# Attention feeding a mixture of experts: turned rows in two buffers, gate columns inside the turning products, loads one by one

## The chip, the cores and the metric

The kernel runs on one core of a Trainium2 chip. The metric is the device time of one execution in microseconds, as the median of several runs. Engines: PE is the matrix engine (its weight loads are listed apart as PEld), DVE the vector engine, ACT the scalar engine, POOL the general engine, SP the engine that issues most DMA transfers. Each runs its own instructions in order, and engines wait for one another by semaphores. PE's array writes to PSUM banks, which DVE and ACT read.

## The reference

Attention over 8 batches, 12 heads, 448 positions and head size 64, with a mix over heads before the softmax and one after it, and then a layer of 8 experts in which each of the 3584 rows goes to the one expert with the largest logit:

```
scores = scale * q @ k.T                                # per batch and head
scores = einsum('bhij,hg->bgij', scores, w_pre)         # mix over heads
attn = softmax(scores)
attn = einsum('bhij,hg->bgij', attn, w_post)            # mix over heads
x = (attn @ v), heads side by side                      # 3584 x 768
logits = x @ w_gate                                     # 8 experts
e = argmax(logits); gate = softmax(logits)[e]
out = gate * (relu(x @ w1[e]) @ w2[e])
```

## The kernel before, in words

**Tiles, blocks and steps.** A batch's 448 queries are cut into four tiles of 120, 120, 120 and 88 queries, 32 tiles in all, and a tile into blocks of up to 20 queries: six blocks in a long tile, five in the short one, 184 in all. The attention stage runs one step per block, 23 steps per batch. What a step does is a list with a sort key for each entry; the list, and so the order on every engine, is written out by the function `at(u, key, what, ...)`, which puts a piece of work into step `u`. A step's pieces come from different tiles, since each tile's work is spread over some twenty steps.

**What one tile goes through.** `load_q` brings its queries (two DMAs of 64 partitions each) and `order_q` reorders them on POOL. `qk` computes the scores of one pair of heads (PE, bank `bs`), and ACT copies them to `si`. Six pairs are done in the six steps from eight steps before the tile's first block on. A short tile has five steps, so once per batch, seven times in all, two pairs fall into one step; the second has the sort key 7, at the step's end. `relayout` (two DMAs on SP, `sb<-si`) puts a block's scores of all heads side by side, three steps ahead of use. `mix` multiplies by the first head matrix (PE, banks `bm`), `top_of` takes the maximum (DVE) and `expo` the exponential (ACT). A step later `weigh` scales the second head matrix (POOL), and two steps later `post` multiplies (56 half records on PE, bank `bp`), and `spread` copies the result to `pt` (DVE). `av` multiplies by v (PE, bank `bx`) over the next tile's steps; `take_a` and `take_b` move its sums to `xt`.

**Turned rows.** `rows` turns `xt` by products with an identity, so that each token is a row, and multiplies it by the gate's columns, with two pairs of heads at a time. So a tile has three visits to `rows`; the first comes three steps after the tile's first `av`. A visit's turned rows stand in columns 360 and up of the two `bx` banks, whose columns below 360 `av` fills; the gate's sums of the three visits stand in the last 24 columns. `copy_x` (ACT, L393) copies turned rows to `xr`, of which there is one buffer, placed between the step's two exponentials. `logits` adds the gate's sums (DVE, L408), `choose` finds the expert, `count` and `dispatch` give each token its place, with a scatter from POOL (L471), and `store_x` writes `xr` to DRAM (`XD`, L399, on SP) in the step before the next tile's first visit.

**Loads.** k of the next batch (six DMAs) comes in steps 2 to 7 of a batch, v in steps 10, 12, 14 and 16, two DMAs each. All these, the q loads, the relayouts and the stores stand in one order on SP.

The expert stage behind it gathers rows by expert from `XD` and runs two layers.

Of the kernel before, what the change touches and what calls it, by code (L numbers as in the profile page):

```python
# [23 lines left out]
P = 128  # L24
# [16 lines left out]
def attn_moe_kernel(ctx, tc, qT, kT, v, w_pre, w_post, w_gate, w1, w2, out):  # L41
# [59 lines left out]
    def load_q(T):  # L101
        b, it, ni = geom[T][:3]
        qr = q_p.tile([P, NPAIR, IT], F32, name="qr", bufs=1)
# [3 lines left out]
        QR[T] = qr  # L107
# [23 lines left out]
    def load_v(b, cs=range(NJ)):  # L131
        for c in cs:
            for r in range(2):
                j0 = min(2 * c + r, NBLK - 1) * D
                nc.sync.dma_start(out=VT[b % 2][r * D:(r + 1) * D, c, :], in_=v[b, j0:j0 + D, :])
# [11 lines left out]
    load_q(0)  # L147
# [42 lines left out]
    wg = const.tile([P, NPAIR, NE], F32, name="wg")  # L190
    nc.scalar.dma_start(out=wg, in_=w_gate.rearrange("(c p) e -> p c e", p=P))
# [175 lines left out]
    LCOL = 512 - 3 * NE  # L367

    def rows(T, pairs, bank, col):
        if 0 in pairs:  # L370
            LG[T] = []
            XR[T] = x_p.tile([IT, NPAIR, 2, D], F32, name="xr")
        to = bank[:, :, col:col + len(pairs) * D].rearrange("p r (c x) -> p r c x", x=D)
        for k, h2 in enumerate(pairs):
            for cs in COLS:
                for r in range(2):
                    rs = slice(r * D, (r + 1) * D)
                    nc.tensor.matmul(out=to[cs, r, k, :], lhsT=xt[rs, h2, cs], rhs=ident[rs, rs],
                                     start=True, stop=True)
        lo = bank[:, :, LCOL + len(LG[T]) * NE:LCOL + (len(LG[T]) + 1) * NE]  # L380
        for k, h2 in enumerate(pairs):
            for cs in COLS:
                for r in range(2):
# [3 lines left out]
        LG[T].append(bank)  # L387


    def copy_x(T, pairs, bank, col):  # L390
        ni = geom[T][2]
        to = bank[:ni, :, col:col + len(pairs) * D].rearrange("p r (c x) -> p c r x", x=D)
        nc.scalar.copy(out=XR[T][:ni, pairs[0]:pairs[-1] + 1], in_=to)  # L393

# [10 lines left out]
    def logits(T):  # L405
        ni, bank, nv = geom[T][2], LG[T][0], len(LG[T])
        lg = LG[T] = sm_p.tile([IT, NE], F32, name="lgs")
        nc.vector.reduce_sum(out=lg[:ni], in_=bank[:ni, :, LCOL:LCOL + nv * NE]  # L408
                             .rearrange("p r (v e) -> p e r v", e=NE), axis=AX.XY)


    def choose(T):
        ni = geom[T][2]
        lg = LG.pop(T)
# [109 lines left out]
    for T in range(NTILE):  # L524
        b, it, ni = geom[T][:3]
        u0, n = ustart[T], len(geom[T][3])
        if T:
            at(max(u0 - QLEAD - 4, -1), 0, load_q, T)
            at(max(u0 - QLEAD - 2, -1), 0.1, order_q, T, 0)
            at(max(u0 - QLEAD - 1, -1), 0.1, order_q, T, 1)  # L530
# [19 lines left out]
        if T == NTILE - 1:  # L550
            O = T - 1

            def whole(T, g, banks):
                for h2 in range(3 * g, 3 * g + 3):
# [5 lines left out]
                    (take_b, T, 0, bank_m), (copy_x, O, (2, 3, 4, 5), bank_x, 0), (logits, O),  # L560
                    (choose, O), (weight, O), (store_x, O), (take_a, T, 1, banks_s),
                    (take_b, T, 1, banks_s), (count, O), (dispatch, O),
                    (rows, T, (0, 1, 2), bank_x, 0), (rows, T, (3, 4, 5), bank_x, 3 * D), (logits, T),
                    (choose, T), (weight, T), (copy_x, T, range(6), bank_x, 0), (store_x, T),
# [17 lines left out]
        for k, pairs in visits:  # L582
# [4 lines left out]
        at(ua + nn + 1, 2.2, logits, T)  # L587
# [4 lines left out]
        at(ua + nn + 2, 5.7, store_x, T)  # L592
# [4 lines left out]
    at(0, 0.5, load_v, 0)  # L597
# [275 lines left out]
```

## Time and profile before

| | us |
|---|---|
| median of 3 runs | 1406.04 |
| lowest and highest | 1405.06, 1407.02 |
| the profiled execution | 1402.59 |
| its span, first to last instruction | 1400.8 |
| PE busy (share of the span) | 1259.6 (90%) |
| DVE, ACT, POOL busy | 735.2 (52%), 657.1 (47%), 389.1 (28%) |

The profile is of one execution, and durations come from it. A busy PE is not a PE at its peak, since matmuls overlap. Idle time of an engine that is not the bottleneck costs nothing, and a share of the whole span averages over stages with different limits, so a stage is read by its own stretch of time. On this profile a step of the attention stage lasts about 3.4 to 10 us, as cut from one `spread` to the next.

### The profile page before, as it was taken

How to read it: one execution, taken by the hardware profiler on the slowest of the kernel's cores; microseconds unless marked ns; L12 is line 12 of the kernel's file. 1: busy time of each engine (PE TensorE's matmuls, PEld its weight loads, DVE VectorE, ACT ScalarE, POOL GpSimd, SP SyncE). 2: the span in 40 equal slices, each digit the busy share in tenths (PEclk: the TensorE clock that was granted, in tenths of full speed). 3: DMA queues.
4: the chain of work that ended last, by engine and by line, in shares of the span. 5: the costliest groups of instructions: out<-in, count | busy, mean ns of one | idle time of the engine just before them, and what ended most of it. 6: DMA issues, size and time to landing. Idle time of an engine off the chain costs nothing. (4 is left out here: it accounts for less than half of the span.)

```text
span 1400.8 us, 57280 instructions
## 1 busy us (share of the span) xinstructions
PE 1259.6 (90%) x25184; PEld 1082.5 (77%) x25184; DVE 735.2 (52%) x1492; ACT 657.1 (47%) x1421; POOL 389.1 (28%) x923
## 2 busy tenths in 40 slices
PE   5889989899888899899899867999999999999995
PEld 1577778777777777687688757989898989988985
DVE  1566757666656675576667655333333333342510
ACT  3556656565655565566566433333333333341510
POOL 3234334333423433343344222202020202020101
PEclk9999999999999999999999887999999999999998
DMA  4663554646536555454634427253433343452501
GB/s 137 185 198 115 172 174 147 182 141 171 170 129 170 153 166 155 135 183 138 184 129 163 144 62 241 77 180 138 132 131 139 125 147 125 140 188 72 165 1 42
DMA packets 116190, 201.21 MB, mean 144 GB/s; under 512 B 40658, under 2 KB 90018, under 8 KB 115924
## 3 DMA queue, kind: packets, MB, share of 16 engines
q1 hardware_dynamic: 108528, 172.38, 39.4%
q0 software_dynamic: 6064, 23.86, 4.6%
q8 instruction: 209, 3.42, 1.0%
q10 hardware_dynamic: 1332, 1.08, 0.3%
q14 instruction: 57, 0.47, 0.1%
HBM read 97.59 MB, written 23.06 MB: 86 GB/s over the span
## 5 line engine op out<-in xcount | busy, mean ns | idle before, releaser
L325 PEld LDWEIGHTS bx<-pt,vt 64*64 64x64 f32 x5952 | 294.4, 136 | 49.4 <-ACT xr L393 38.8
L252 PE MATMUL bm<-sb,Wpre 64*64 64x448 f32 x1440 | 325.8, 556 | 5.4 <-DMA sb<-si 4.6
L325 PE MATMUL bx<-pt,vt 64*64 64x120 f32 (+3 forms) x5952 | 302.2, 253 | 30.5 <-ACT xr L393 27.5
L258 DVE TENSOR_REDUCE st<-bm 128x1 f32<-128x448 f32 (+1 forms) x368 | 225.9, 623 | 162.8 <-PE bm L252 136.5
L264 ACT ACTIVATE et<-bm,st 128x448 f32<-128x448 f32 (+1 forms) x368 | 233.1, 636 | 93.8 <-DVE st L258 89.9
L295 PE MATMUL bp<-wp,et 60*64 60x60 f32 x10080 | 231.2, 225 | 30.4 <-issue 29.5
L306 DVE COPY pt<-bp 128x960 f32<-128x960 f32 (+1 forms) x184 | 216.3, 1175 | 73.9 <-PE bp L295 70.2
L295 PEld LDWEIGHTS bp<-wp,et 60*64 60x64 f32 x10080 | 207.1, 138 | 41.6 <-issue 38.6
L226 PE MATMUL bs<-kr,qq 64*64 64x448 f32 (+1 forms) x1536 | 207.1, 576 | 23.0 <-ACT si L228 13.2
L228 ACT COPY si<-bs 120x896 f32<-120x896 f32 (+1 forms) x192 | 173.6, 904 | 101.6 <-PE bs L226 99.5
L277 POOL TENSOR_SCALAR wp<-Wpost,st 128x60 f32<-128x60 f32 (+1 forms) x368 | 110.4, 312 | 301.3 <-DVE st L274 222.9
L729 POOL DMA_INDIRECT out<-y,ti x30 | 33.7, 1122 | 455.4 <-ACT xh L656 339.7
L252 PEld LDWEIGHTS bm<-sb,Wpre 64*64 64x64 f32 x1440 | 94.4, 138 | 84.0 <-issue 52.4
L701 PE MATMUL pm_h<-xh,ah 128*128 128x512 f32 (+1 forms) x384 | 146.0, 380 | 1.6 <-PEq L753 0.7
L701 PE MATMUL pm_h<-xl,ah 128*128 128x512 f32 (+1 forms) x384 | 145.1, 378 | 0.0
L701 PE MATMUL pm_h<-xh,al 128*128 128x512 f32 (+1 forms) x384 | 145.0, 378 | 0.0
L720 PE MATMUL pm_y<-bh,hh 128*128 128x384 f32 x480 | 127.8, 343 | 0.0
L720 PE MATMUL pm_y<-bl,hh 128*128 128x384 f32 x480 | 123.6, 336 | 0.0
L720 PE MATMUL pm_y<-bh,hl 128*128 128x384 f32 x480 | 121.1, 336 | 0.0
L705 DVE SCALAR_TENSOR_TENSOR hl<-pm_h,hh 128x512 fp32r<-128x512 f32 (+1 forms) x64 | 42.0, 657 | 134.5 <-ACT hh L704 134.4
L704 ACT ACTIVATE hh<-pm_h 128x512 fp32r<-128x512 f32 (+1 forms) x64 | 36.5, 571 | 147.9 <-PE pm_h L701 147.7
L725 DVE TENSOR_SCALAR y<-pm_y,tb 128x384 f32<-128x384 f32 x30 | 18.4, 614 | 155.4 <-PE pm_y L720 155.4
(106 smaller groups left out, 1626.8 us busy)
## 6 DMA issues: line engine op xcount, KB each, us to landing
sb<-si SPq DMA_DIRECT2D x360, 210.0 KB
wraw<-in_w SPq DMA_DIRECT2D x64, 384.0 KB
wraw<-in_w SPq DMA_DIRECT2D x46, 512.0 KB
vt<-in_v SPq DMA_DIRECT2D x64, 192.0 KB
kr<-in_kT SPq DMA_DIRECT2D x48, 224.0 KB
qr<-in_qT SPq DMA_DIRECT2D x48, 180.0 KB
XD<-xr SPq DMA_DIRECT2D x24, 360.0 KB
qr<-in_qT SPq DMA_DIRECT2D x16, 132.0 KB
```

The lines of the kernel that those rows point to most:

```text
L226: nc.tensor.matmul(out=bank_s[cs, r, :S], lhsT=QQ[T][hs, c, cs], rhs=KR[b, c][hs, :], start=True, stop=True)
L228: nc.scalar.copy(out=SI[T][:ni, 2 * c:2 * c + 2, :], in_=bank_s[:ni, :, :S])
L252: nc.tensor.matmul(out=bank_m[x][c * D:(c + 1) * D, :S], lhsT=Wpre[hs, :], rhs=SB[T, s][hs, c, :], start=True, stop=True)
L258: nc.vector.reduce_max(out=st[:top, 0, x:x + 1], in_=bank_m[x][:top, :S], axis=AX.X, negate=True)
L264: nc.scalar.activation(out=et[:top, x, :], in_=bank_m[x][:top, :S], func=AF.Exp, bias=st[:top, 0, x:x + 1], scale=1.0, accum_out=st[:top, ...
L277: nc.gpsimd.tensor_scalar(out=wp[:top, x, :], in0=Wpost[:top], scalar1=st[:top, 2, x:x + 1], scalar2=1.0, op0=ALU.mult, op1=ALU.mult)
L295: nc.tensor.matmul(out=bank_p[g * D:(g + 1) * D, n, o:o + nw], lhsT=et[hs, x, j * D:(j + 1) * D], rhs=wp[hs, x, :], start=True, stop=True)
L306: nc.vector.tensor_copy(out=to, in_=src[:, :2 * nh])
L325: nc.tensor.matmul(out=o, lhsT=VT[b % 2][rs, c, h * D:(h + 1) * D], rhs=i, start=(c == 0), stop=(c == NJ - 1))
L701: nc.tensor.matmul(out=ph[:, :n], lhsT=wx[:, fs], rhs=xx[:, kt, :n], start=(m == 0), stop=(m == 3 * NK1 - 1))
L705: nc.vector.scalar_tensor_tensor(out=hl[:, ft, :n], in0=ph[:, :n], scalar=0.0, in1=hh[:, ft, :n].bitcast(F32), op0=ALU.max, op1=ALU.subtract)
L720: nc.tensor.matmul(out=py[g][:, :384], lhsT=hx[:, kt, ts], rhs=wx[:, g * 384:(g + 1) * 384], start=(n == 0), stop=(n == 3 * NK2 - 1))
```

## The change

It has four parts. (1) `xr` gets two buffers, and `store_x` comes two steps later for all tiles but the last three. (2) `rows` multiplies by one operand `iw`, which holds 64 identity columns and 8 gate columns for each pair of heads, so a turning product has 72 columns and the gate's own products are gone. The gate's columns stand beside each pair's turned columns; `logits` adds them at each visit, and `choose` adds the three results. Two POOL copies fill `iw` at the start. (3) The loads of k, v and q are placed in single pieces: k in steps 1, 3, 4, 8, 9 and 12, v in steps 12, 13, 14, 15, 18, 20, 20 and 21, the halves of q in two steps, the first a step earlier than before. (4) The second score pair of a step gets the key 0.96 and so stands ahead of the step's mixes.

```diff
-    def load_q(T):
+    def load_q(T, half):
...
-        for half in range(2):
-            nc.sync.dma_start(out=qr[half * D:(half + 1) * D, :, :ni], in_=src[half])
+        nc.sync.dma_start(out=QR[T][half * D:(half + 1) * D, :, :ni], in_=src[half])
...
-    wg = const.tile([P, NPAIR, NE], F32, name="wg")
-    nc.scalar.dma_start(out=wg, in_=w_gate.rearrange("(c p) e -> p c e", p=P))
+    iw = const.tile([P, NPAIR, D + NE], F32, name="iw")
+    nc.scalar.dma_start(out=iw[:, :, D:], in_=w_gate.rearrange("(c p) e -> p c e", p=P))
+    for r in range(2):
+        rs = slice(r * D, (r + 1) * D)
+        nc.gpsimd.tensor_copy(out=iw[rs, :, :D],
+                              in_=ident[rs, rs].unsqueeze(1).to_broadcast([D, NPAIR, D]))
...
-            XR[T] = x_p.tile([IT, NPAIR, 2, D], F32, name="xr")
+            XR[T] = x_p.tile([IT, NPAIR, 2, D], F32, name="xr", bufs=2)
+            LG[T] = sm_p.tile([IT, NE, 3], F32, name="lg")
...
-                    nc.tensor.matmul(out=to[cs, r, k, :], lhsT=xt[rs, h2, cs], rhs=ident[rs, rs],
+                    nc.tensor.matmul(out=to[cs, r, k, :], lhsT=xt[rs, h2, cs], rhs=iw[rs, h2, :],
                                      start=True, stop=True)
-        lo = bank[:, :, LCOL + len(LG[T]) * NE:LCOL + (len(LG[T]) + 1) * NE]
-        for k, h2 in enumerate(pairs):
-            for cs in COLS:
-                for r in range(2):
-                    rs = slice(r * D, (r + 1) * D)
-                    nc.tensor.matmul(out=lo[cs, r, :], lhsT=xt[rs, h2, cs], rhs=wg[rs, h2, :],
-                                     start=(k == 0), stop=(k == len(pairs) - 1))
...
+    def logits(T, v, n, bank, col):
+        ni = geom[T][2]
+        nc.vector.reduce_sum(out=LG[T][:ni, :, v], in_=turned(bank, col, n)[:ni, :, :, D:]
+                             .rearrange("p r c e -> p e r c"), axis=AX.XY)
...
+        lg = sm_p.tile([IT, NE], F32, name="lgs")
+        nc.vector.reduce_sum(out=lg[:ni], in_=lg3[:ni, :, :nv], axis=AX.X)
...
-            at(max(u0 - QLEAD - 4, -1), 0, load_q, T)
...
+                at(max(u0 - QLEAD - 5 + half, -1), 0.01 * T, load_q, T, half)
...
-            for c in range(NPAIR):
-                at(u0 + 2 + c, 5.6, load_k, b + 1, c)
-            for c in range(NJ):
-                at(u0 + 10 + 2 * c, 5.6, load_v, b + 1, (c,))
+            for c, k in enumerate((1, 3, 4, 8, 9, 12)):
+                at(u0 + k, 5.6, load_k, b + 1, c)
+            for c, k in enumerate((12, 13, 14, 15, 18, 20, 20, 21)):
+                at(u0 + k, 5.6, load_v, b + 1, (c,))
...
-            at(u, 7 if u in scored and u >= 0 else 5, qk, T, c)
+            at(u, 0.96 if u in scored and u >= 0 else 5, qk, T, c)
...
+            at(ua + k, 2.2, logits, T, n3, 2, bank_x, 3 * IT)
...
-        at(ua + nn + 2, 5.7, store_x, T)
+        at(ua + nn + (4 if T < NTILE - 3 else 2), 5.7, store_x, T)
```

The order on SP, steps 10 to 15 of the third batch, before. `vt` are loads of v, `qr` of q, `sb` the relayouts and `XD` the store; x2 means two DMAs.

```order
L135 DMA vt_114<-in_v 64x768 x2
L106 DMA qr<-in_qT 64x6x120 x2
L238 DMA sb_161<-si 120x1x448 x2
L399 DMA XD<-xr 88x768
L238 DMA sb_162<-si 120x1x448 x2
L135 DMA vt_114<-in_v 64x768 x2
L238 DMA sb_163<-si 120x1x448 x2
L238 DMA sb_164<-si 120x1x448 x2
```

And in the change, from step 11 of the same batch on:

```order
L106 DMA qr<-in_qT 64x6x120
L242 DMA sb_161<-si 120x1x448 x2
L242 DMA sb_162<-si 120x1x448 x2
L98 DMA kr<-in_kT 128x448
L134 DMA vt_114<-in_v 64x768
L242 DMA sb_163<-si 120x1x448 x2
L134 DMA vt_114<-in_v 64x768
L404 DMA XD<-xr 88x768
L242 DMA sb_164<-si 120x1x448 x2
L134 DMA vt_114<-in_v 64x768
```

The store of the short tile moved two relayouts back, and no two DMAs of v stand side by side here.

PE where two score pairs fall into one step, before (third such place, buffer numbers shown), right behind `post`: the second half of the last pair of the short tile, then the next tile's first pair, then the next step's mix and its `av`.

```order
L226 MATMUL bs_95<-kr_2505,qq_4479 64x448
L226 MATMUL bs_95<-kr_2505,qq_4479 56x448
L226 MATMUL bs_95<-kr_4038,qq_4922 64x448
L226 MATMUL bs_95<-kr_4038,qq_4922 56x448
L226 MATMUL bs_95<-kr_4038,qq_4922 64x448
L226 MATMUL bs_95<-kr_4038,qq_4922 56x448
L252 MATMUL bm0_107<-sb2_163,Wpre_156 64x448 x2
L325 MATMUL bx_103<-pt_4518,vt0_113 64x120 x6
```

And in the change:

```order
L230 MATMUL bs_95<-kr_2594,qq_4329 64x448
L230 MATMUL bs_95<-kr_2594,qq_4329 56x448
L230 MATMUL bs_95<-kr_3823,qq_4754 64x448
L230 MATMUL bs_95<-kr_3823,qq_4754 56x448
L230 MATMUL bs_95<-kr_3823,qq_4754 64x448
L230 MATMUL bs_95<-kr_3823,qq_4754 56x448
L256 MATMUL bm0_107<-sb1_162,Wpre_156 64x448 x2
L329 MATMUL bx_103<-pt_4368,vt0_113 64x120 x6
```

Both times the next tile's pair (`kr_4038`, `kr_3823`) stands right behind another pair; in the change it is the last pair but one of the short tile, a step earlier, as the relayout buffer of the mix behind shows (`sb1` for `sb2`).

DVE from a tile's last visit to its choice of the expert, before:

```order
L258 TENSOR_REDUCE st_1213<-bm1_111 128x1
L274 RECIPROCAL st_1123<-st_1123 128x2
L408 TENSOR_REDUCE lgs_1260<-bx_103 120x8
L306 COPY pt_1083<-bp_99 128x4x48x5
L417 MAX m8_1291<-lgs_1260 120x8
```

And in the change, where the second row of the logits' three stands in the step before:

```order
L397 TENSOR_REDUCE lg_914<-bx_103 120x8
L310 COPY pt_1077<-bp_99 128x4x48x5
L262 TENSOR_REDUCE st_1202<-bm0_107 128x1
L262 TENSOR_REDUCE st_1202<-bm1_111 128x1
L278 RECIPROCAL st_1116<-st_1116 128x2
L397 TENSOR_REDUCE lg_914<-bx_103 120x8
L310 COPY pt_1077<-bp_99 128x4x48x5
L414 TENSOR_REDUCE lgs_1271<-lg_914 120x8
L417 MAX m8_1273<-lgs_1271 120x8
```

One reduce of the logits (L397) stands ahead of each visit's `spread` (L310), and one more (L414) behind the last.

## Rows read from the trace of the kernel before

**Rows 1.** The page of the profile, its first part: the span, and each engine's busy time, share of the span and instructions.
```profile
span 1400.8 us, 57280 instructions
...
PE 1259.6 (90%) x25184; PEld 1082.5 (77%) x25184; DVE 735.2 (52%) x1492; ACT 657.1 (47%) x1421; POOL 389.1 (28%) x923
```

**Rows 2.** Busy time in stretches of the attention stage: the stretch, its length, busy us of PE, PE's weight loads, DVE, ACT and POOL with instruction counts, granted clock of TensorE as a share of full speed, share of the DMA engines, GB/s. The last line sums all five.
```profile
35.00:232.00 197.00, 175.90 (x5294) 143.26 (x5294) 127.99 (x273) 118.22 (x281) 71.94 (x201) 0.96 0.56 169
...
731.00:816.00 85.00, 75.13 (x2550) 66.57 (x2544) 59.47 (x138) 46.51 (x120) 31.58 (x92) 0.94 0.42 132
sum 781.00, PE 700.54 PEld 582.05 DVE 515.45 ACT 464.84 POOL 295.66; mean PE 140.11 PEld 116.41 DVE 103.09 ACT 92.97 POOL 59.13
```

**Rows 3.** Who waited for whom, PE's own waits: line that waited, what it waited for, us in total, times, longest. "issue" is time in which the engine waited for nothing that the profile shows.
```profile
PE bp L295 <- issue: 29.5, 56, 2.3
PE bx L325 <- ACT xr L393: 27.5, 13, 4.5
...
PE bs L226 <- ACT si L228: 13.2, 13, 1.1
...
PE bx L385 <- issue: 5.5, 11, 0.8
```

**Rows 4.** The same view for ACT, the wait before the copy of turned rows.
```profile
ACT xr L393 <- DMA XD<-xr: 71.2, 17, 7.2
```

**Rows 5.** The timeline around one such wait: start, us, engine, line, operation, count, and in brackets the idle time ahead of it and what ended it.
```profile
574.03 0.47 SPq L399 DMA_DIRECT2D XD<-xr  x1
...
575.36 0.81 POOL L124 COPY qq<-qr 128x360 f32<-128x360 f32 x1 [0.91 <-DMA qr<-in_qT]
...
579.86 0.37 ACT L393 COPY xr<-bx 120x256 f32<-120x256 f32 x1 [7.23 <-DMA XD<-xr]
...
580.29 1.44 PE L325 MATMUL bx<-pt,vt 64*64 64x120 f32 x18 [4.48 <-ACT xr L393]
...
581.46 0.97 PE L252 MATMUL bm<-sb,Wpre 64*64 64x448 f32 x2
...
584.98 0.54 PE L252 MATMUL bm<-sb,Wpre 64*64 64x448 f32 x2
```

**Rows 6.** Busy time in the thirteen stretches, each from one `spread` (L306) to the next, that hold the thirteen waits of PE for the copy of turned rows (first, last and sum; columns as in rows 2).
```profile
150.62:157.93 7.31, 5.48 (x108) 4.23 (x104) 2.53 (x5) 2.92 (x7) 0.70 (x4) 0.77 0.87 240
...
791.24:801.03 9.79, 5.36 (x102) 4.77 (x102) 2.39 (x4) 2.34 (x7) 1.13 (x5) 0.55 0.68 214
sum 88.02, PE 60.45 PEld 45.80 DVE 32.66 ACT 36.06 POOL 11.75; mean PE 4.65 PEld 3.52 DVE 2.51 ACT 2.77 POOL 0.90
```

**Rows 7.** The same view of the two like stretches in the last batch, where no such wait stands.
```profile
746.73:749.77 3.04, 3.04 (x108) 2.67 (x104) 2.52 (x4) 2.63 (x7) 0.19 (x1) 1.00 0.66 240
769.12:772.27 3.15, 3.15 (x108) 2.79 (x104) 2.52 (x5) 2.17 (x6) 0.19 (x1) 1.00 0.70 209
```

**Rows 8.** The same view of a step without such a wait at the third place, and of one with a visit to `rows`.
```profile
302.72:306.12 3.40, 3.40 (x108) 2.92 (x104) 2.52 (x4) 2.71 (x7) 1.14 (x3) 1.00 0.42 149
161.03:164.57 3.54, 3.54 (x140) 3.18 (x136) 2.52 (x6) 3.01 (x9) 2.50 (x8) 1.00 0.02 5
```

**Rows 9.** PE's timeline at one visit to `rows`: turning products (L378), gate products (L385), then `post` (L295). Records are half matmuls, two for each. The last line is the view by source line of all gate records: duration min, median and max in ns, first and last start, forms.
```profile
417.68 0.44 PE L378 MATMUL bx<-ident,xt 64*56 64x64 f32 x14
417.92 0.42 PE L385 MATMUL bx<-wg,xt 64*64 64x8 f32 x16
418.17 0.94 PE L295 MATMUL bp<-wp,et 60*64 60x60 f32 x49
...
L385 PE MATMUL bx<-wg,xt x1536: 166/199/221, 75.3 to 828.0; 64*64 64x8 f32 x118, 64*56 64x8 f32 x74
```

**Rows 10.** DVE by line and form (busy us, mean ns of one, idle ahead): reduces of the logits over 48 and 32 numbers, and of 8 numbers. The last line is DVE's wait of `spread` for `post`.
```profile
L408 DVE TENSOR_REDUCE lgs<-bx 120x8 f32<-120x48 f32 x23 | 4.8, 208 | 6.3 <-ACT xr L393 5.7
...
L469 DVE TENSOR_REDUCE sc<-pos 120x1 f32<-120x8 f32 x24 | 3.9, 161 | 0.8
...
L408 DVE TENSOR_REDUCE lgs<-bx 88x8 f32<-88x32 f32 x1 | 0.2, 187 | 2.2 <-PE bx L385 2.2
...
DVE pt L306 <- PE bp L295: 70.2, 104, 3.6
```

**Rows 11.** Busy time in seventeen stretches from `spread` to `spread` that hold the choice of the expert (first, last, sum with mean; columns as in rows 2).
```profile
142.43:145.84 3.41, 3.41 (x112) 2.92 (x108) 3.31 (x12) 2.53 (x8) 1.06 (x6) 1.00 0.73 244
...
717.32:720.77 3.45, 3.45 (x110) 3.14 (x105) 3.35 (x11) 2.25 (x8) 0.94 (x5) 1.00 0.77 223
sum 58.56, PE 58.56 PEld 51.68 DVE 56.77 ACT 40.50 POOL 17.45; mean PE 3.44 PEld 3.04 DVE 3.34 ACT 2.38 POOL 1.03
```

**Rows 12.** The timeline around one scatter of POOL (L471).
```profile
744.15 1.09 POOL L471 DMA_INDIRECT TB<-tg,di  x1 [1.38 <-issue]
...
744.93 0.34 PE L295 MATMUL bp<-wp,et 60*64 60x60 f32 x3 [0.34 <-issue]
...
745.91 0.72 PE L295 MATMUL bp<-wp,et 60*64 60x60 f32 x23 [0.65 <-issue]
```

**Rows 13.** The timeline at a second score pair: PE's scores behind the `si` copy.
```profile
592.28 0.90 ACT L228 COPY si<-bs 90x896 f32<-90x896 f32 x1 [0.73 <-PE bs L226]
...
593.23 0.98 PE L226 MATMUL bs<-kr,qq 64*64 64x448 f32 x8 [1.01 <-ACT si L228]
```

**Rows 14.** What SP's DMA queue waited for, its largest wait.
```profile
SPq L238 <- ACT si L228: 298.0, 32, 14.1
```

More of the change, by code (lines that the diff above doesn't have):

```diff
@@ L99, in load_k @@
         KR[b, c] = kr
-    def load_q(T):
+    def load_q(T, half):
         b, it, ni = geom[T][:3]
-        qr = q_p.tile([P, NPAIR, IT], F32, name="qr", bufs=1)
+        if half == 0:
+            QR[T] = q_p.tile([P, NPAIR, IT], F32, name="qr", bufs=1)
         src = qT[b, :, H * it * IT:H * (it * IT + ni)].rearrange("d (c t i) -> t d c i", c=NPAIR, t=2)
-        for half in range(2):
-            nc.sync.dma_start(out=qr[half * D:(half + 1) * D, :, :ni], in_=src[half])
-        QR[T] = qr
+        nc.sync.dma_start(out=QR[T][half * D:(half + 1) * D, :, :ni], in_=src[half])
     def order_q(T, part):
@@ L129, in attn_moe_kernel, with load_v @@
     VT = [p.tile([P, NJ, HD], F32, name=f"vt{n}") for n, p in enumerate(v_p)]
-    def load_v(b, cs=range(NJ)):
-        for c in cs:
-            for r in range(2):
-                j0 = min(2 * c + r, NBLK - 1) * D
-                nc.sync.dma_start(out=VT[b % 2][r * D:(r + 1) * D, c, :], in_=v[b, j0:j0 + D, :])
+    def load_v(b, blocks=range(2 * NJ)):
+        for k in blocks:
+            c, r = divmod(k, 2)
+            j0 = min(k, NBLK - 1) * D
+            nc.sync.dma_start(out=VT[b % 2][r * D:(r + 1) * D, c, :], in_=v[b, j0:j0 + D, :])
     w12 = const.tile([P, 2, H], F32, name="w12")
@@ L146, in attn_moe_kernel @@
     nc.scalar.activation(out=warm, in_=warm, func=AF.Exp)
-    load_q(0)
+    for half in range(2):
+        load_q(0, half)
     order_q(0, 0)
@@ L364, in attn_moe_kernel, with turned @@
     XR, LG = {}, {}
-    LCOL = 512 - 3 * NE
+    DW = D + NE
+    def turned(bank, col, n):
+        return bank[:, :, col:col + n * DW].rearrange("p r (c x) -> p r c x", x=DW)
     def rows(T, pairs, bank, col):
         if 0 in pairs:
-            LG[T] = []
-            XR[T] = x_p.tile([IT, NPAIR, 2, D], F32, name="xr")
-        to = bank[:, :, col:col + len(pairs) * D].rearrange("p r (c x) -> p r c x", x=D)
+            XR[T] = x_p.tile([IT, NPAIR, 2, D], F32, name="xr", bufs=2)
+            LG[T] = sm_p.tile([IT, NE, 3], F32, name="lg")
+        to = turned(bank, col, len(pairs))
         for k, h2 in enumerate(pairs):
@@ L377, in rows @@
                     rs = slice(r * D, (r + 1) * D)
[L378 removed]
+                    nc.tensor.matmul(out=to[cs, r, k, :], lhsT=xt[rs, h2, cs], rhs=iw[rs, h2, :],
                                      start=True, stop=True)
[L380 to L387 removed]
     def copy_x(T, pairs, bank, col):
         ni = geom[T][2]
[L392 removed]
+        to = turned(bank, col, len(pairs))[:ni, :, :, :D].rearrange("p r c x -> p c r x")
         nc.scalar.copy(out=XR[T][:ni, pairs[0]:pairs[-1] + 1], in_=to)
+    def logits(T, v, n, bank, col):
+        ni = geom[T][2]
+        nc.vector.reduce_sum(out=LG[T][:ni, :, v], in_=turned(bank, col, n)[:ni, :, :, D:]
+                             .rearrange("p r c e -> p e r c"), axis=AX.XY)
     def store_x(T):
@@ L403, in attn_moe_kernel @@
     DD = {}
[L405 to L409, printed above, removed]
     def choose(T):
         ni = geom[T][2]
-        lg = LG.pop(T)
+        lg3, nv = LG.pop(T), 2 if T >= NTILE - 2 else 3
+        lg = sm_p.tile([IT, NE], F32, name="lgs")
+        nc.vector.reduce_sum(out=lg[:ni], in_=lg3[:ni, :, :nv], axis=AX.X)
         m8 = sm_p.tile([IT, NE], F32, name="m8")
@@ L559, in attn_moe_kernel @@
                     (rows, O, (2, 3, 4, 5), bank_x, 0), (whole, T, 1, banks_s), (take_a, T, 0, bank_m),
-                    (take_b, T, 0, bank_m), (copy_x, O, (2, 3, 4, 5), bank_x, 0), (logits, O),
-                    (choose, O), (weight, O), (store_x, O), (take_a, T, 1, banks_s),
+                    (take_b, T, 0, bank_m), (copy_x, O, (2, 3, 4, 5), bank_x, 0),
+                    (logits, O, 1, 4, bank_x, 0), (choose, O), (weight, O), (store_x, O), (take_a, T, 1, banks_s),
                     (take_b, T, 1, banks_s), (count, O), (dispatch, O),
-                    (rows, T, (0, 1, 2), bank_x, 0), (rows, T, (3, 4, 5), bank_x, 3 * D), (logits, T),
-                    (choose, T), (weight, T), (copy_x, T, range(6), bank_x, 0), (store_x, T),
+                    (rows, T, (0, 1, 2), bank_x, 0), (rows, T, (3, 4, 5), bank_x, 3 * DW),
+                    (logits, T, 0, 3, bank_x, 0), (logits, T, 1, 3, bank_x, 3 * DW), (choose, T), (weight, T), (copy_x, T, range(6), bank_x, 0), (store_x, T),
                     (count, T), (dispatch, T)]
@@ L581, in attn_moe_kernel @@
             at(ua + k, 2.1, take_b, T, g, banks_x)
-        for k, pairs in visits:
+        for n3, (k, pairs) in enumerate(visits):
+            at(ua + k, 2.2, logits, T, n3, 2, bank_x, 3 * IT)
             at(ua + k, 1.3, rows, T, pairs, bank_x, 3 * IT)
@@ L586, in attn_moe_kernel @@
             continue
-        at(ua + nn + 1, 2.2, logits, T)
         at(ua + nn + 1, 4.4, choose, T)
@@ L596, in attn_moe_kernel @@
             at(u, 1, phases, mixed, pairs_at.get(u, []))
-    at(0, 0.5, load_v, 0)
+    at(0, 0.9, load_v, 0)
     with tc.manual_schedule():
```

4 lines of the change are left out of this document (2 added, 2 removed).

## The prediction, made before the change was run

> **What bounds the kernel now.** I read the page's busy table, then stretches of the span, then who waited for whom, then single steps. The PE is busy for 90% of the span, no other engine above 52% [rows 1]. Five stretches from 35 to 816 us hold the attention stage: PE 90%, DVE 66%, ACT 60% of it [rows 2]. The expert stage behind it is untouched by the change. In attention work comes in 184 steps of one block each, so the question is what lengthens a step.
>
> The longest PE waits there are four [rows 3]: 29.5 us in 56 waits of `post` (L295) on "issue", 27.5 us in 13 waits of `av` (L325) on the copy `xr` (L393, ACT), 13.2 us of `qk` (L226) on the copy `si`, and 5.5 us on issue at the gate products (L385). The second is a chain: ACT itself waited 71.2 us in 17 waits for the store of the earlier tile's turned rows [rows 4]. One case: SP issues the store at 574.03, ACT gets the buffer at 579.86 after 7.23 us, PE goes on at 580.29 after 4.48 us, and its next mix pair shows 0.97 us where 0.54 us is usual [rows 5]. PE does not wait for the copy's data. It waits because the copy reads the bank that the next `av` writes, and because the second exponential stands behind the copy on ACT.
>
> **Part 1, two buffers for the turned rows, store two steps later.** Thirteen stretches, each from one `spread` to the next, hold the 13 PE waits: 88.02 us together [rows 6]. The same places in the last batch, where nothing waited, took 3.04 and 3.15 us [rows 7]. The thirteenth has its like in a step of about 3.4 us [rows 8]. So 88.0 - (12 x 3.10 + 3.4) = 47.4 us are excess. [...] With two buffers the copy waits for the store of two tiles back. By the schedule that store is issued four to five steps before the copy, some 14 to 17 us at 3.4 us a step, against a longest wait of 7.2 us. Bounds: 25 us (about the listed wait alone) to 50. I take **-45**, close to the excess, since the reference is the same code.
>
> **Part 2, gate columns inside the turning products.** 1536 gate records go [rows 9]; the 1536 turning records get 72 columns instead of 64. A visit runs 16 of each: from 417.92 to 418.17, so 0.25 us for the gate's 16; the 14 turning records before them took 0.24, or 0.27 for 16 [rows 9]. 96 x 0.25 = 24 us. Twelve per cent more columns on 0.27 us cost at most 0.04 a visit, some 3.5 us. Visit steps are the PE's: 3.54 us of PE with DVE busy 2.52 and ACT 3.01 [rows 8], so the saving shows. Bounds 0 (another engine closes in) to -24; I take **-20**. [...]
>
> **Part 3, the logits.** One DVE reduction a tile (208 ns) becomes three of at least 187 ns and one more over 24 numbers, priced at 0.165 from the 8-number reduce of 161 ns [rows 10]: +0.52 us a tile, 16.6 us in 32 tiles. The three lie in visit steps, ahead of `spread`, which itself waits for PE's `post` (70.2 us in 104 waits [rows 10]); there they are hidden. The extra one stands in the step of the choice, where DVE is busy 3.34 of 3.44 us on average over 17 such steps [rows 11]: 30 x 0.165 = **+5**. Bounds 0 to 16.6. [...]
>
> **Part 4, the loads.** Their number and bytes stay; they come one per step and not two. PE's waits on "issue" at L295 and L385 are 35.0 us [rows 3]. Some lie right behind POOL's scatter L471: it starts at 744.15, PE stops for 0.34 and 0.65 us up to 745.91 [rows 12]. A scatter comes once per tile, and this one lies in the last batch, which loads nothing for a next one: such waits stay. At 0.65 us a tile, between the two, they are 21 of the 35. The other 14 may come from bursts of loads; nothing here proves it. Bounds 0 to -35; I take half of the 14, **-7**. A later load of k or v costs nothing while it lands before its use: the last of k is issued 8 steps, the last of v 11 steps ahead.
>
> **Part 5, the second score pair first.** The order shows two score groups back to back on PE before and after, only one step earlier. The wait for the `si` copy (1.01 us at 593.23 [rows 13]) moves with them, seven times. The copy now stands ahead of the exponentials and overwrites a buffer that relayouts of the tile two back still read; SP's FIFO decides when these land. Bounds -7 to +15 (ACT late by 2 us, seven times); **0**. The two new POOL copies at the start cost about 1.6 us (two of 0.8, as a `qq` copy [rows 5]) beside scores that are paced by ACT until 26 us: 0.
>
> **The sum.** The profiled execution took 1402.59 us. -45 - 20 + 5 - 7 = -67 gives 1335.6. The median of the runs lies 3.45 us above that execution, so **1339**. The likeliest case's own range is 1322 to 1356.
>
> **Rivals.**
> - *The issue waits go as well* (17%): they come from bursts and from the number of PE records. The last batch, without loads, has clean steps, which speaks for it; the waits beside the scatter speak against. All 35 instead of 7: 1311.
> - *The gain is half given back* (18%): without the stall the steps are bound by DVE (3.34 of 3.44 in choice steps) or by ACT's wait on `si`; the relayouts, which SP held back 298.0 us for ACT [rows 14], become late as steps shorten. Only the listed 27.5 us and half the gate's 20 come back, less 5: -32, so 1374. Against it: DVE at 66%.
> - *The buffer still isn't free* (4%): the store is stuck in SP's queue for over five steps, so the second buffer doesn't do what it says. Only gates, loads and logits count, -22: 1384.
> - *Slower, one mechanism* (4%): the logits hold the bank. `rows` writes the same columns of `bank_x` and the next `av` the same bank, so PE now also waits for DVE at each visit. Each wait must cost 67 / 96 = 0.70 us to eat the gain, and 0.75 would end at about 1411. Against it: in the third visit this wait exists already and is not among PE's longer ones; `post` and `qk` lie between.
>
> **Numbers.** Likeliest 56%, rivals 17, 18, 4 and 4%, no visible change 1%. A run of this kernel can tell about 0.2% (2.8 us). Faster 95%, same 1%, slower 4%. The range 1306 to 1374 takes in the first two rivals' times and the bounds of the loads; left out are the tails beyond, the third and the slower one.
>
> **What would show it.** Right: ACT's wait for XD gone or under 10 us; no step over 6 us at these places; 1536 PE records fewer and a visit's PE time shorter by about 0.2 us; the 1 us waits on `si` still seven; issue waits by the scatter still there once a tile. Wrong: new waits of `av` on the DVE logits, of `si` copies on relayouts, of mixes on `sb`, or choice steps well over 3.6 us.

## The result, and the profile of the changed kernel

The changed kernel takes 1353.24 us (median of 4 runs, 1344.39 to 1355.88) against 1406.34 us (the kernel before had four runs by then): a ratio of 0.9612 with an interval of 0.9568 to 0.9657, 53 us less. Forecast were 1339 us, and 1322 to 1356 for the likeliest case. Direction and range held; 14 us of the forecast gain did not come. Its profiled execution took 1355.88 us, the longest of the four. Here and below medians are of all runs of a kernel, and ratios leave out runs in a slower state, more than 1.5% above its fastest. The page of the changed kernel, span and busy time of the engines and the row of a DMA queue that brings instructions (packets, MB, share of 16 engines):

```profile
span 1354.1 us, 54310 instructions
...
PE 1228.0 (91%) x23648; PEld 1064.7 (79%) x23648; DVE 741.7 (55%) x1586; ACT 659.5 (49%) x1421; POOL 390.0 (29%) x925
...
q8 instruction: 197, 3.23, 1.1%
```

PE shed 1536 matmul records against [rows 1]. The two stages apart, cut at the last `spread` (columns as in [rows 2]), in the changed kernel:

```profile
36.77:761.29 724.52, 666.03 (x20362) 561.96 (x20356) 520.56 (x1239) 467.30 (x1121) 297.13 (x812) 0.98 0.57 169
761.29:1354.10 592.81, 539.98 (x3128) 496.75 (x3128) 215.89 (x332) 178.55 (x279) 77.83 (x72) 0.95 0.36 124
```

The same cut of the kernel before, from a second profile of it (1401.6 us; taken with the experiments):

```profile
36.41:817.46 781.05, 712.32 (x21824) 588.73 (x21818) 513.64 (x1149) 464.40 (x1121) 295.75 (x812) 0.96 0.53 157
817.46:1401.60 584.14, 535.59 (x3206) 494.12 (x3200) 215.43 (x329) 179.02 (x279) 77.55 (x72) 0.97 0.36 125
```

The attention stage gave 56.5 us. The expert stage, which the change does not touch, gave 8.7 back. Who waited for whom in the attention stage of the changed kernel (columns as in [rows 3]):

```profile
PE bp L299 <- issue: 29.6, 35, 2.5
PE bs L230 <- ACT si L232: 12.0, 10, 3.0
PE bx L329 <- issue: 8.0, 9, 1.7
...
ACT si L232 <- DMA sb<-si: 19.8, 5, 5.8
```

PE's wait for the copy `xr` and ACT's wait for the store [rows 3, 4] are gone. The waits on "issue" are no shorter, 37.6 us in these two lines alone, where the two of [rows 3] have 35.0, and `qk` waits 12.0 us for the `si` copy, where [rows 3] has 13.2 in the whole span and 7.0 in the attention stage.

Steps of like place in the eight batches, summed, tell where the 56.5 us came from. Places are counted in steps of a batch, 0 to 22. First the steps of the thirteen waits and the dispatch steps ahead of them (3, 4, 9, 10, 15, 16), in the kernel before, second profile:

```profile
sum 246.43, PE 205.14 PEld 165.85 DVE 132.19 ACT 121.32 POOL 95.37; mean PE 4.27 PEld 3.46 DVE 2.75 ACT 2.53 POOL 1.99
...
sum 92.69, PE 89.94 PEld 76.00 DVE 64.48 ACT 59.88 POOL 19.66; mean PE 3.75 PEld 3.17 DVE 2.69 ACT 2.50 POOL 0.82
...
sum 117.53, PE 112.01 PEld 94.56 DVE 106.20 ACT 76.29 POOL 35.45; mean PE 3.50 PEld 2.96 DVE 3.32 ACT 2.38 POOL 1.11
...
sum 72.71, PE 64.48 PEld 52.42 DVE 41.94 ACT 49.15 POOL 20.77; mean PE 4.03 PEld 3.28 DVE 2.62 ACT 3.07 POOL 1.30
```

The other lines there are plain visit steps (1, 7, 19, each with a tile's third visit), choice steps (2, 8, 14, 20) and the two steps around the second score pair (12, 13). The same four sums in the changed kernel:

```profile
sum 177.43, PE 167.93 PEld 142.88 DVE 131.46 ACT 114.72 POOL 93.14; mean PE 3.50 PEld 2.98 DVE 2.74 ACT 2.39 POOL 1.94
...
sum 85.19, PE 82.86 PEld 72.64 DVE 63.80 ACT 58.20 POOL 17.40; mean PE 3.45 PEld 3.03 DVE 2.66 ACT 2.42 POOL 0.73
...
sum 120.55, PE 112.94 PEld 95.09 DVE 110.26 ACT 88.45 POOL 41.30; mean PE 3.53 PEld 2.97 DVE 3.45 ACT 2.76 POOL 1.29
...
sum 82.24, PE 69.66 PEld 55.04 DVE 42.07 ACT 46.26 POOL 17.77; mean PE 4.35 PEld 3.44 DVE 2.63 ACT 2.89 POOL 1.11
```

So -69.0 at the thirteen waits, -7.5 in plain visits, +3.0 in choices, +9.5 at the second pair, and +7.5 in all remaining steps: -56.5. At the places that the prediction named the gain is larger than forecast; three other places took some back, the last of them, as counted below, with more waits at block edges.

### The profile page after: what moved, and what is told of

Read it like the earlier page. It is cut to its first block, busy times and chain, and to the rows that moved or that the text cites. A ratio compares the mean times of both kernels' runs of the same rounds, so it can differ in the third digit from the quotient of the medians.

```text
span 1354.1 us, 54310 instructions
## 1 busy us (share of the span) xinstructions
PE 1228.0 (91%) x23648; PEld 1064.7 (79%) x23648; DVE 741.7 (55%) x1586; ACT 659.5 (49%) x1421; POOL 390.0 (29%) x925
## 5 line engine op out<-in xcount | busy, mean ns | idle before, releaser
L256 PE MATMUL bm<-sb,Wpre 64*64 64x448 f32 x1440 | 322.3, 554 | 4.6 <-DMA sb<-si 3.8
L299 PE MATMUL bp<-wp,et 60*64 60x60 f32 x10080 | 227.9, 223 | 32.1 <-issue 29.6
L310 DVE COPY pt<-bp 128x960 f32<-128x960 f32 (+1 forms) x184 | 216.0, 1174 | 40.5 <-PE bp L299 35.4
L299 PEld LDWEIGHTS bp<-wp,et 60*64 60x64 f32 x10080 | 202.9, 136 | 42.3 <-issue 36.7
L256 PEld LDWEIGHTS bm<-sb,Wpre 64*64 64x64 f32 x1440 | 97.3, 137 | 76.1 <-issue 39.9
```

Of the source, the lines that this page charges most:

```text
L256: nc.tensor.matmul(out=bank_m[x][c * D:(c + 1) * D, :S], lhsT=Wpre[hs, :], rhs=SB[T, s][hs, c, :], start=True, stop=True)
L299: nc.tensor.matmul(out=bank_p[g * D:(g + 1) * D, n, o:o + nw], lhsT=et[hs, x, j * D:(j + 1) * D], rhs=wp[hs, x, :], start=True, stop=True)
L310: nc.vector.tensor_copy(out=to, in_=src[:, :2 * nh])
```

## Experiments

The kernels ran in three groups, each on a chip of its own. Each ratio is to runs of the kernel before on the same chip; that kernel's medians were 1402.0, 1402.1 and 1401.5 us, with single times from 1391 to 1418, so 0.5% either way stays open, more than the 0.2% that the prediction reckoned with.

**First group: the change again, two parts alone, the pair undone.**

Unaltered (`again`):

> The changed kernel once more, unaltered. In its first profile the attention stage (first spread to last spread) took 724.5 us where the kernel before took 781.0, but the expert stage behind it, which the change does not touch, took 592.8 where it took 583.6. Theory: those 9 us are chance (one gather of the expert rows waited 6.6 us, and the granted clock fell behind it); then this profile shows an expert stage that differs by several us from 592.8, and single times scatter over 1344 to 1356. Rival: the shorter attention stage makes the expert stage longer, since its weights and rows come sooner after it; then the stage takes 590 us or more again, with the long gather at the same place, and the time is within 2 us of 1353.

1349.8 us (1338.9 to 1358.0), ratio 0.9613 (0.9558 to 0.9668). The expert stage took 593.9 us, the long gather at its place: chance falls.

Two buffers alone, on the kernel before:

```
-            XR[T] = x_p.tile([IT, NPAIR, 2, D], F32, name="xr")
+            XR[T] = x_p.tile([IT, NPAIR, 2, D], F32, name="xr", bufs=2)
```

> The kernel before with nothing changed but two buffers for the turned rows; the store stays where it was. Theory: the thirteen stretches with the wait go back from 88.0 to about 40 us, PE's 27.5 us of waits for the copy are gone, and the time is 45 to 51 us lower, 1355 to 1361. Rival: the steps that held the wait also served as slack for relayouts and loads, so new waits take about half of it: 1375 to 1385. If the store two relayouts later is needed as well, ACT still waits for the store more than 20 us in sum.

1378.9 us, ratio 0.9833 (0.9785 to 0.9881): -23 us, half. At the waits the whole gain is there. Sum of the six places in this kernel:

```profile
sum 201.25, PE 178.63 PEld 149.90 DVE 132.36 ACT 123.57 POOL 97.29; mean PE 3.72 PEld 3.12 DVE 2.76 ACT 2.57 POOL 2.03
```

246.4 - 201.3 = 45.2 us, the -45 of the prediction, and no wait for the store is left. But the attention stage fell only from 781.1 to 753.1 us, so 17.2 us came back in the other steps. Its two largest waits on "issue":

```profile
PE bp L295 <- issue: 30.0, 37, 2.9
...
PE bx L325 <- issue: 12.5, 12, 2.0
```

In the second profile of the kernel before, the stall and the same two lines:

```profile
PE bx L325 <- ACT xr L393: 29.6, 14, 3.6
PE bp L295 <- issue: 14.9, 24, 1.7
...
PE bx L325 <- issue: 2.6, 4, 1.1
```

So the stall had covered another one. What that one is, can be read by counting. PE's stream of instructions was counted through in the trace, in order of start (a weight load and a matmul are one each, semaphores and branches too); these are waits on "issue" of the changed kernel:

```
end of wait, us   length, us   line   number of the waiting instruction   modulo 256
  72.94           0.44         L299    1986                               194
  77.97           1.32         L299    2242                               194
  82.47           0.77         L299    2498                               194
 152.25           1.76         L299    6339                               195
 412.63           2.48         L299   20931                               195
 739.86           2.14         L299   40131                               195
```

All 37 such waits of 0.25 us or more in its attention stage have 194 or 195 there. Six kernels, same count:

```
kernel                        blocks of 256   waits on issue      of them at a block's edge
                              in attention    >= 0.25 us, sum     number, sum
before, second profile        171.6           22.3                31   22.3
two buffers alone             171.6           45.8                48   45.8
changed, but old gates        171.6           52.9                56   52.6
changed                       160.2           36.3                37   36.3
changed, but old loads        160.2           28.5                35   27.9
changed, but pair last        160.2           41.1                43   40.5
```

So in these six kernels PE's waits on "issue" stand, with few exceptions, where a block of 256 instructions ends and the next has to be there. The page's instruction queue fits: 209 packets with 3.42 MB before, 16.4 kB each; the changed kernel has 12 packets fewer, and its stream in the whole trace is 3071 instructions shorter, 12.0 blocks. A fifth to a third of the edges stop PE in these six kernels, by up to 2.5 us in the changed one.

With two buffers alone half of the edge waits are new (45.8 against 22.3 us), and they account for most of what came back: outside the six places they rise from 11.9 to 25.8 us, 13.9 of the 17.2.

The packets of that queue tell what PE waits for. In these six kernels exactly one packet lands for each block, and all 250 stops, short and long, end 1.1 to 1.9 us after a packet has landed; no edge is crossed less than 0.9 us after one. In the changed kernel the packet ahead of a stop starts 2.2 us (median) after the edge before, at the other edges 1.2, while PE's blocks take 3.8 and 4.1 us (medians, without the stop). By these times the next block comes barely in time, and one that starts late stops PE; a PE that stands still inside a block for another reason seems to give it time to land (22.3 us of edge waits with the copy's stall, 45.8 without). What makes a packet late is shown in part only: in the two us from 0.3 us behind the earlier edge on, the DMA engines are 72% busy ahead of the stops of the changed kernel and 51% ahead of the other edges.

Gate columns alone, with their logits, on the kernel before:

```
-                    nc.tensor.matmul(out=to[cs, r, k, :], lhsT=xt[rs, h2, cs], rhs=ident[rs, rs],
+                    nc.tensor.matmul(out=to[cs, r, k, :], lhsT=xt[rs, h2, cs], rhs=iw[rs, h2, :],
...
-                    nc.tensor.matmul(out=lo[cs, r, :], lhsT=xt[rs, h2, cs], rhs=wg[rs, h2, :],
```

> The kernel before with nothing changed but the gate columns inside the turning products and the logits that belong to them (one buffer for the turned rows, the old places of store, loads and second pair). Theory: visit steps go from 3.54 to about 3.31 us, choice steps rise from 3.44 to 3.65, steps with a dispatch fall a little, the thirteen waits stay; together 12 to 16 us less, 1390 to 1394. Rival: the fall of the dispatch steps from 4.9 to 4.2 us that the changed kernel shows (30 of them, 21 us) belongs to this part, since PE's waits on issue stood behind the gate products there; then 25 to 33 us less, 1373 to 1381.

1408.7 us (12 runs), ratio 1.0023 (0.9977 to 1.0070): nothing, against both theories. Its attention stage took 776.8 us, 4.3 less than in the second profile of the kernel before, and its expert stage 592.0, 7.9 more. The waits of its chain, of ACT, DVE and PE:

```profile
ACT xr L392 <- DMA XD<-xr: 93.5, 29, 5.9
...
DVE lg L397 <- ACT xr L392: 93.5, 87, 5.2
...
PE bx L329 <- DVE lg L397: 54.2, 23, 4.8
```

The chain is the old one with a link more: the store is late, ACT's copy waits for it, the new reduce on DVE follows that copy, and `av` waits for the reduce because both use the bank. Here the rival "the logits hold the bank" is real.

Second pair last again, the rest as changed:

```
-            at(u, 0.96 if u in scored and u >= 0 else 5, qk, T, c)
+            at(u, 7 if u in scored and u >= 0 else 5, qk, T, c)
```

> The changed kernel with the second score pair of a step back at the end of its step. Theory: placed first it costs time, because ACT's copy of the second pair waits up to 3.6 us for relayouts to free the buffer, ahead of the exponentials; PE's waits for the si copy fall from 12.0 to 7 us, ACT's wait for that DMA (19.8 us) goes below 5, and the time is 3 to 8 us lower, 1345 to 1350. Rival: it is worth nothing either way, or the early place helps: the same within 2 us, or 3 us higher, 1351 to 1357.

1343.9 us (1338.9 to 1352.6), ratio 0.9586 (0.9536 to 0.9635), 6 us under `again` on the same chip. The intervals overlap, so the total is a hint. The place itself is clearer: steps 12 and 13 sum to

```profile
sum 70.81, PE 63.19 PEld 50.50 DVE 42.72 ACT 46.44 POOL 15.68; mean PE 3.95 PEld 3.16 DVE 2.67 ACT 2.90 POOL 0.98
```

where `again` has 80.8. In the six profiles with two buffers and the pair first these steps take 78 to 82 us, with the pair last 70.8 to 72.7 in four and 81.1 and 83.8 in the first profile of the kernel before and in two buffers alone. Those two hold stops at block edges of up to 2.3 and 2.9 us ahead of the pair, and the step behind ran at a granted clock of 0.65 and 0.55; there the stop and what followed it cost more than the stop's length. In two buffers alone, the two steps of the batch with the 2.9 us stop, and the second one of a batch without:

```profile
364.19:371.42 7.23, 4.33 (x140) 3.84 (x136) 2.52 (x4) 2.52 (x6) 1.49 (x5) 0.85 0.46 115
371.42:380.40 8.98, 7.99 (x148) 5.45 (x144) 2.73 (x5) 3.53 (x7) 0.60 (x2) 0.55 0.42 141
180.25:185.94 5.69, 4.68 (x148) 3.40 (x144) 2.73 (x6) 3.21 (x6) 0.70 (x3) 1.00 0.47 156
```

The timeline of the changed kernel shows how the 10 us arise:

```profile
454.99 0.98 PE L230 MATMUL bs<-kr,qq 64*64 64x448 f32 x8 [0.99 <-ACT si L232]
...
458.50 0.91 ACT L232 COPY si<-bs 120x896 f32<-120x896 f32 x1 [3.56 <-DMA sb<-si]
459.31 0.64 ACT L268 ACTIVATE et<-bm,st 128x448 f32<-128x448 f32 x1
459.46 0.98 PE L230 MATMUL bs<-kr,qq 64*64 64x448 f32 x8 [0.81 <-ACT si L232]
```

The early pair still waits 0.99 us [rows 13]. Its copy then waits 3.56 us for relayouts to leave the `si` buffer, and the exponentials, whose reduces DVE began at 456.86, stand behind it on ACT.

**Second group: gates undone, loads undone, the pair in the middle, the kernel before.**

Separate gate products as before, the rest as changed:

```
-                    nc.tensor.matmul(out=to[cs, r, k, :], lhsT=xt[rs, h2, cs], rhs=iw[rs, h2, :],
+                    nc.tensor.matmul(out=to[cs, r, k, :], lhsT=xt[rs, h2, cs], rhs=ident[rs, rs],
...
+                    nc.tensor.matmul(out=lo[cs, r, :], lhsT=xt[rs, h2, cs], rhs=wg[rs, h2, :],
```

> The changed kernel with separate gate products and one logits reduce a tile, as before; two buffers, late store, early second pair and spread loads stay. Theory: gate columns with their logits are worth 12 to 18 us here, because nothing waits for the store any more: attention 733 to 740 us, time 1362 to 1369; visit steps back at 3.54 us and choice steps at 3.44. Rival: they are worth 25 to 35 (the steps with a dispatch, which hold the third visit, go back from 4.2 to 4.9 us): 1375 to 1385. Second rival: worth nothing, as alone on the kernel before: 1347 to 1354.

1372.0 us (1365.2 to 1383.3), ratio 0.9766 (0.9725 to 0.9808). By this ratio and that of `again`, from two chips, gate columns with their logits are worth 1.5%, 21 us, between theory and rival. Its profile is of the slowest of its six runs, 1383.3 us, so sums from it may come out high. Visit steps 1, 7, 19:

```profile
sum 97.75, PE 90.57 PEld 76.61 DVE 64.29 ACT 59.31 POOL 18.70; mean PE 3.77 PEld 3.19 DVE 2.68 ACT 2.47 POOL 0.78
```

That is 12.6 us over the changed kernel in 24 steps, twice the 0.25 us of the products [rows 9]. 4.9 of them are waits at block edges (6.9 against 2.1 us in these steps, 52.6 against 36.3 in the stage); what is left is 0.32 us a visit. Its choice steps sum to 120.0 us and those of the changed kernel to 120.6: the extra reduce costs next to nothing.

Loads back at their old places:

```
-            for c, k in enumerate((12, 13, 14, 15, 18, 20, 20, 21)):
-                at(u0 + k, 5.6, load_v, b + 1, (c,))
+            for c in range(NJ):
+                at(u0 + 10 + 2 * c, 5.6, load_v, b + 1, (2 * c, 2 * c + 1))
...
```

> The changed kernel with the loads of k, v, q and the reordering of q back at their old places. The second buffer alone brought the attention stage from 781.0 to 753.1 us, the whole change without the early second pair to 711.2, so gate columns, loads and the later store share 42 us. Theory: gate columns are worth about 15 of them as summed, so the spread loads are worth 20 to 27: here the attention stage takes 738 to 748 us and the time is 1368 to 1376, with more issue waits than 38 us. Rival: the loads are worth the 7 us of the prediction and the gate columns the rest: attention 726 to 732, time 1354 to 1360.

1337.7 us (1333.3 to 1350.6), ratio 0.9548 (0.9498 to 0.9599): against both. Spreading the loads brings no gain; the old places look better by 0.65%, but the intervals overlap and the chips differ.

The pair between turning products and `post`:

```
-            at(u, 0.96 if u in scored and u >= 0 else 5, qk, T, c)
+            at(u, 2.5 if u in scored and u >= 0 else 5, qk, T, c)
```

> The changed kernel with the second score pair in the middle of its step, after the mix, av and turning products and ahead of post, so that a whole post lies between it and the step's own pair, and on ACT its copy stands behind the exponentials. Theory: the wait for the si copy was 7 us with the pair last (7 times 1.0) and 12 us with it first; here it falls below 3 us, ACT's wait for the relayouts no longer blocks the exponentials, and the time is 4 to 8 us lower than with the pair last, 1336 to 1341. Rival: the copy delays the bank for the pair at the end of the step or the next exponentials, and the step is as long as with the pair last: 1342 to 1348.

1342.9 us (1340.9 to 1348.5), ratio 0.9577 (0.9537 to 0.9617); the rival. The stall only moved: the pair at the step's end now waits for the other's copy, 14.7 us in 7 times:

```profile
PE bs L230 <- ACT si L232: 14.7, 7, 3.2
```

The kernel before once more:

> The kernel before once more, for its stages: in its first profile the expert stage (behind the last spread) took 583.6 us, in all five other profiles so far, of two kernels with and three without most of the change, 591 to 594. Theory: the 583.6 were a favourable execution, and this profile shows 588 to 594 as well. Rival: it shows 583 to 585 again; then every one of the edits, the second buffer alone too, costs the expert stage 8 to 10 us.

Its expert stage took 584.1 us, as in the first profile, so the 7 to 10 us more of `again`, of the two-buffer kernel and of the other kernels with gate columns in these two groups are real; with old gates it took 587.3, and in the third group the three kernels with two buffers have 588.9 to 590.8. One part can be placed. PE's first products behind the second gather of rows (L654), and the scatter on POOL that the gather stands behind; in the kernel before, last `spread` at 817.16:

```profile
902.74 1.00 POOL L729 DMA_INDIRECT out<-y,ti  x1 [2.92 <-ACT xh L656]
...
910.42 0.85 PE L654 MATMUL pm_x<-ident,xs 128*128 128x128 f32 x6 [1.47 <-DMA xs<-XD,tcl]
```

In the changed kernel, last `spread` at 761.29:

```profile
849.63 1.65 POOL L729 DMA_INDIRECT out<-y,ti  x1 [4.43 <-DVE al L489]
...
858.77 1.51 PE L654 MATMUL pm_x<-ident,xs 128*128 128x128 f32 x6 [6.58 <-DMA xs<-XD,tcl]
```

From the last `spread` the scatter starts after 85.6 and 88.3 us, and PE waits 5.1 us longer. In the 30 us from 80 us behind the last `spread` on, PE is busy 22.2 to 23.5 us in all ten profiles of kernels with gate columns and 27.2 to 27.8 in the four without, so this part goes with the gate columns. Why is not shown, nor where the second buffer alone loses its 7 us.

**Third group, on a chip that showed more waits on "issue".** Its kernels have 9 to 13 us of them away from block edges; 31 to 35 waits of each kernel start within 2.3 us of the scatter L471, as in the first profile of the kernel before [rows 12], where the changed kernel's profile has 5. The kernel before showed 18.9 us of such waits in that profile and 8.3 in its second, so they don't come from an edit, and this group is read within itself.

Pair last and old loads, the two edits shown above together:

> The changed kernel with two of its edits undone at once: the second score pair last and all loads at their old places. Theory: the two losses are separate, 6 us for the early pair and 12 us for the new places of the loads, and add up: 1349.8 - 18 gives 1328 to 1335, the lowest of all. Rival: both end in the same slack (a wait of ACT or of PE on issue that one of them already took away), then no better than with the old loads alone: 1336 to 1342.

1349.2 us (1340.9 to 1356.5), ratio 0.9629 (0.9583 to 0.9674). Not lower than either edit alone; the sum of two gains did not show. Of the four parts only two buffers (with the later store) and gate columns are left in this kernel, and it has the whole gain of the change, 52 us by its ratio.

Old places for k and v alone:

```
-            for c, k in enumerate((1, 3, 4, 8, 9, 12)):
-                at(u0 + k, 5.6, load_k, b + 1, c)
+            for c in range(NPAIR):
+                at(u0 + 2 + c, 5.6, load_k, b + 1, c)
...
```

> The changed kernel with the loads of k and v back at their old places, while the loads of q stay in two steps, with their later reordering on POOL. Theory: the 12 us that the new places cost lie with k and v, whose single pieces now stand among the relayouts of SP's queue at the tile boundary: 1336 to 1342. Rival: they lie with q: 1347 to 1353.

1352.6 us (1344.2 to 1360.5), ratio 0.9650 (0.9603 to 0.9697).

The store at its old place:

```
-        at(ua + nn + (4 if T < NTILE - 3 else 2), 5.7, store_x, T)
+        at(ua + nn + 2, 5.7, store_x, T)
```

> The changed kernel with the store of the turned rows back at its old place, two relayouts earlier in SP's queue; two buffers stay. Theory: with two buffers the place does not matter, since ACT's copy waits for the store of two tiles back in either case: the same within 3 us, 1346 to 1353. Rival: the later place keeps relayouts ahead of the store in SP's queue and is worth 4 us or more: 1354 or above.

1353.7 us (1346.0 to 1362.3), ratio 0.9680 (0.9639 to 0.9722). These three cannot be told apart, nor from the changed kernel: places of loads and store are worth less than this measurement sees.

One buffer in the changed kernel:

```
-            XR[T] = x_p.tile([IT, NPAIR, 2, D], F32, name="xr", bufs=2)
+            XR[T] = x_p.tile([IT, NPAIR, 2, D], F32, name="xr")
```

> The changed kernel with one buffer for the turned rows; the store stays two relayouts later. Theory: the copy waits for the store again, two steps longer than before, and PE's av waits behind the logits as it did with the gate columns alone (54 us): 55 to 80 us more, 1400 to 1430, while PE's waits on issue fall from 37 to under 25 us, because PE stands still anyway. Rival: gate columns and loads leave room so that the buffer is worth only the 23 us that it is worth alone: 1368 to 1378.

1608.5 us (1607.5 to 1613.4), ratio 1.1486 (1.1427 to 1.1545), far beyond both. Two of its waits, of ACT and of PE:

```profile
ACT xr L392 <- DMA XD<-xr: 259.5, 29, 11.6
...
PE bx L329 <- DVE lg L397: 200.3, 29, 10.0
```

The store now stands two relayouts later, a step behind the next tile's first visit, whose copy waits for it; so each copy waits longer, and each wait reaches PE through the logits. The granted clock falls as well, to 0.895 over the span, where the changed kernel has 0.968. Waits at block edges fall to 7.8 us in it. The second buffer is worth 23 us alone, some 55 beside gate columns (ratios 1.0023 without it and 0.9629 with it and the later store, on two chips), and some 250 where the store comes late.

No kernel clearly beats the changed one; with old loads, or with the pair last or in the middle, the medians are lower, with overlapping intervals.

## Why the prediction held, and where it was off

- **The chain at the copy** was right, and so was its price at the place: 45.2 us measured with two buffers alone. The step that failed is "I take -45, close to the excess, since the reference is the same code". The excess ended, but 17 of the 45 us came back in other steps, 13.9 of them as waits at block edges, and the run gained 23. The stall had covered these waits; the last batch, taken as reference, could not show that.
- **Gate columns.** 0.25 us a visit was about the right size: plain visit steps fell by 7.5 us in 24, 0.31 each; the four other places with a visit and no second pair or wait (0, 6, 18, 21) fell by 2.2 us in 32, by 7.3 when waits at block edges are left out. Undone in the changed kernel, gate columns and logits together are worth 21 us, where -20 and +5 make 15. What was not seen is that this needs the second buffer: alone they gave nothing.
- **Logits.** +5 was forecast; choice steps rose by 3.0 against the kernel before and by 0.6 against the same kernel with old gates. The slower rival had a true mechanism: 54 us of waits for the reduce with one buffer, 200 with the later store as well. With two buffers PE shows none, and ACT's copy, ahead of the reduce, no longer waits for the store.
- **Loads and issue.** The cause that was named is not borne out. Waits on "issue" stand at block edges and, in some profiles, beside the scatter; in the profile that the prediction read, 21.6 of 36.4 us (waits of 0.25 us or more) are at edges, a term that it did not have. Busy DMA engines go with the stops (72% busy ahead of those of the changed kernel, 51% ahead of its other edges), but single loads left more of them than the old places, 36.3 against 27.9 us. The 7 us were not found; the undone loads were, if anything, faster.
- **Second pair.** 0 was taken from bounds of -7 to +15; the place cost about 10 us in these profiles, the run perhaps 6, by the mechanism behind the upper bound.
- **Not in the sum:** 9 us in the expert stage, which was called untouched.
- Of the marks named, five held: no wait for XD, no long step at these places, 1536 records fewer, shorter visits, seven 1 us waits on `si` (with three more, up to 3.0). One failed: waits beside the scatter nearly vanished from this profile. One of the warnings came true, `si` copies waiting for relayouts.

The rival "half given back" named a wrong cause (DVE or relayouts) for a thing that did happen to the second buffer. The rival "the issue waits go as well" named the number of PE's records, and 11 blocks fewer do go with less waiting at edges (52.6 and 45.8 us in the two kernels with two buffers and old gates, 36.3 in the changed one); but the waits did not go, they grew from 22.3.

That the sum came near is luck in part. The prices of the two main parts, -60 with the logits, were summed as if each stood for itself; alone they gave 23 us and nothing, together 52. Of the 14 us that are missing some 8 lie there, and 7 are the loads.

## What to carry to other kernels

Before a stall is booked as gain, look for waits that it covers: here waits at block edges rose from 22.3 to 45.8 us when 30 us of PE's stalls went. Where PE waits on "issue" in the middle of a run of equal products, count its instructions; if the waits stand a multiple of 256 apart, as here, look at when the packets of its instruction queue land; here fewer instructions went with less of it, and moved loads did not help. And test parts in pairs: here one part was worth nothing without the other, and the other more than twice as much beside it.

## What the runs showed of the hardware

- PE stopped at edges of 256 instructions: 31 to 56 of 160 to 172 edges for 0.25 us or more in the six kernels above, 22 to 53 us in an attention stage, the longest 1.9 to 2.9 us, with one 16 kB packet of the instruction queue per block; each stop ended 1.1 to 1.9 us after a packet had landed.
- With two buffers alone, a stop of 2.9 us at such an edge was followed by a step of 8.98 us at a granted clock of 0.55; in a batch without the stop the same step took 5.7 us at 1.00.
- Short waits on "issue" beside POOL's scatter change with the chip, it seems: within 2.3 us of its start the kernels of the third group have 14 to 16 us of them, the changed kernel 3 to 4 in two profiles, the kernel before 18.9 in one profile and 8.3 in the other, at equal attention stages (781.0 and 781.1 us).
